# SwiGLU feed-forward on one core: chunks 1 to 3 computed together, each gate and up weight block loaded once for three matmuls, full array in place of column pairs

## The chip, the core and the metric

The kernel runs on one core of a Trainium2 chip. TensorE (PE) multiplies; a weight load (PEld) puts a stationary block into its array, a matmul streams up to 512 columns past it. ScalarE (ACT) computes the SiLU, VectorE (DVE) the products and most copies, SyncE (SP) issues nearly all transfers. The metric is the device time of one execution in microseconds; before the change it is 120.16 us (median of 3 runs, 119.78 to 120.52).

## What is computed

`out = (silu(x @ w_gate) * (x @ w_up)) @ w_down`, in bf16 with fp32 sums, for 2048 tokens, a model width D of 512 and an inner width F of 1376:

```python
B, S, D, F = 1, 2048, 512, 1376
g = _silu(x @ w_gate)      # (2048, 1376)
u = x @ w_up               # (2048, 1376)
return (g * u) @ w_down    # (2048, 512)
```

## The kernel before

**Tiles.** Tokens come in four chunks of 512, the inner width in ten blocks of 128 and a rest of 96. A *group* is one result of 128 inner columns by one chunk's 512 tokens, held in one of the 8 PSUM banks and summed over four matmuls (D is four blocks of 128, index `dk`). Kind G is a gate block, U an up block. X (one for each chunk) holds the last 96 gate columns and the last 32 up columns; Y (one for a pair of chunks) holds 64 more up columns of two chunks. That makes 20 G and U groups and one X for each chunk, then two Y: 86 groups. The down projection follows, with groups O, one for each 128 tokens.

**Banks.** Groups are numbered in order and group n uses bank n mod 8. Before TensorE starts a group it waits until every reader of group n - 8 is done (`free`).

**Column pairs.** `whole` issues one matmul of a group. At the start it uses the full array: one load of 128x128 and one matmul. From the fifth group on, `in_pairs` is true, and the work is issued as two halves side by side: two loads of 128x64 at column positions 0 and 64, two matmuls, each with half of the outputs and the same moving data. The Y groups use such halves too (L432), and the down projection (L470) uses four strips of 32 rows side by side. The rest of the last four token tiles (L506) is in the full array again: one load and one matmul of 128x128 for each inner block.

**Order on TensorE.** Warm-up matmuls, transposes of the first two token tiles, the first 8 groups (chunk 0, inner blocks 0 to 3) in slices of 128 and 256 tokens as x arrives, then the groups in number order: the rest of chunk 0, its X, chunk 1 (20 groups and X), chunk 2, chunk 3, both Y. Then the down projection starts. Its quads are four O groups each: a quad's step is four strip matmuls with different rows of the inner dimension. `strips(0, 0, ...)` runs ten such steps on the first four O groups, `strips(1, 0, ...)` the same on the next four. At its start a quad waits for the four banks to be free: those of the first quad were last used by groups 78 to 81 of 86, those of the second by 82 to 85.

**Readers.** For each pair (chunk, block), ACT writes silu(G) to `sg_sb` and DVE multiplies that by U into `hT_sb`. An X group has three readers: ACT writes 32 rows to `sgx_sb` and 64 rows to `sgy_sb`, and DVE makes `hx_sb` from `sgx_sb`. A Y group is read by one DVE product, which needs `sgy_sb` of both of its chunks. ACT and DVE each run their operations in the order in which they were planned.

**Transfers.** SP issues, in this order, a tile of x, the gate and up slabs with two transposing loads of x for the second half of chunk 0 among them, then one transposing load (`DMA_TRANSPOSE`, L95) for each of chunks 1, 2 and 3, then w_down. TensorE waits for chunk c's load before its first group of chunk c (`gu_needs`).

Of the kernel before, what the change touches and what calls it, by code (L numbers as in the profile page):

```python
# [14 lines left out]
def bass_standalone__swiglu_ffn__prompt_kernel(nc, x, w_gate, w_up, w_down, out):  # L15
    _, S, D = x.shape
    F = w_gate.shape[1]
    P = 128
    KD = D // P
    NFF = F // P  # L20
    NFT = NFF + 1
    F_LAST = F - NFF * P
    SC = 512
    NSC = S // SC
# [5 lines left out]
    HT = SC // 2  # L30
    NXN = HT // P
    NB = 8
    NSG = 4
    NOS = 8
    SR = 32
    PW = 64
# [2 lines left out]
    Y_ROWS = [0, 64, 0, 64]  # L39
    X_ROWS = [64, 0, 96, 32]  # L40
    ORDER = [1, 2, 3, 0]
    assert D == 512 and S % SC == 0 and KD == 4 and F_LAST == 96 and NSC % 2 == 0

    xf = x[0]
# [3 lines left out]
    UPH = F + 32  # L48
    WTOT = 2 * F
    XC0 = NFF * P  # L50
    YC0 = UPH + NFF * P

    with ExitStack() as es:
# [7 lines left out]
        hT_sb = sb("hT_sb", [P, NFF, S], BF16)  # L61
# [3 lines left out]
        adummy = sb("act_dummy", [P, 8], FP32)  # L65
        sg_sb = [sb(f"sg_sb{i}", [P, SC], FP32) for i in range(NSG)]
        sgx_sb = [sb(f"sgx_sb{c}", [P, SC], FP32) for c in range(NSC)]
# [10 lines left out]
        s_P = sem("s_P")  # L78
# [70 lines left out]
        groups = []  # L149
# [3 lines left out]
        def add_group(kind, **what):  # L153
            g = dict(kind=kind, at=len(groups), bank=banks[len(groups) % NB], readers=[], **what)
            groups.append(g)
            return g

        def add_op(eng, g, **what):
            n_read[eng] += 1
            op = dict(g=g, at=n_read[eng], **what)  # L160
            (act_ops if eng == "A" else dve_ops).append(op)
            g["readers"].append((eng, op["at"]))
            return op

        def tview(i, dk):
            return banks[KD * i + dk][:, 0:P // 2].bitcast(BF16)

        sg_reader = []
        n_sg = 0
        h_ready = {}  # L170

        def plan_pair(c, ft):
            nonlocal n_sg
            gg = add_group("G", c=c, ft=ft)
            gu = add_group("U", c=c, ft=ft)
            b = n_sg % NSG
            free = sg_reader[n_sg - NSG] if n_sg >= NSG else 0
            a = add_op("A", gg, kind="silu", out=sg_sb[b][:, :], src=gg["bank"][:, :], free=free)
            d = add_op(
                "D", gu, kind="mul", out=hT_sb[:, ft, c * SC:(c + 1) * SC], a=sg_sb[b][:, :],  # L180
                b=gu["bank"][:, :], after=a["at"],
            )
            sg_reader.append(d["at"])
            h_ready[c] = d["at"]
            n_sg += 1

        def yblk(c):
            return (0, 64) if c % 2 == 0 else (64, 128)
# [4 lines left out]
        def plan_x(c):  # L193
            g = add_group("X", c=c)
            y0, y1 = yblk(c)
            add_op("A", g, kind="silu", out=sgx_sb[c][96:128, :], src=g["bank"][64:96, :], free=0)
            a = add_op("A", g, kind="silu", out=sgy_sb[c // 2][y0:y1, :], src=g["bank"][0:64, :], free=0)
            d = add_op(
                "D", g, kind="mul", out=hx_sb[X_ROWS[c]:X_ROWS[c] + SR, c, :],
                a=sgx_sb[c][96:128, :], b=g["bank"][96:128, :], after=a["at"] - 1,  # L200
            )
            y_after[c // 2] = a["at"]
            t_ready[c] = d["at"]
# [10 lines left out]
        for i in range(NXN):  # L214
            for dk in range(KD):
# [3 lines left out]
                    out=xT_sb[:, dk, i * P:(i + 1) * P], src=tview(i, dk), stored=(None, 0),  # L219
                )  # L220
                xt_ready[i, dk] = (eng, op["at"])

        for c in range(NSC):
            for ft in range(NFF):
                plan_pair(c, ft)
            plan_x(c)
        for pi in range(NSC // 2):
            plan_y(pi)
# [3 lines left out]
        n_store = [0] * NOS  # L232
        tiles = [c * TPC + q for q in range(TPC) for c in ORDER]
        for at, t in enumerate(tiles):
            ob = at % NOS
            if at == 2 * TPC:
                parted = add_op(
                    "D", dict(readers=[]), kind="copy", ready=(s_T, N_TURNS), out=part_sb[:, :],
                    src=banks[(NO + NST - 1) % NB][:, LASTH:D], stored=(None, 0),
# [4 lines left out]
            for c0, c1 in parts:  # L244
                g = add_group("O", t=t, c0=c0, c1=c1)
# [66 lines left out]
        def on_tensor(pe):  # L312
            landed = set()

            def need(name, count=1):
                if name not in landed:
                    pe.wait_ge(loads[name], 16 * count)
                    landed.add(name)
# [3 lines left out]
            def after(eng, n):  # L322
                if n > read[eng]:
                    pe.wait_ge(s_A if eng == "A" else s_D, n)
                    read[eng] = n

            def free(g):
                if g["at"] >= NB:
                    for eng, n in groups[g["at"] - NB]["readers"]:
                        after(eng, n)  # L330

            in_pairs = False

            def whole(bank, dk, col, c, n0, n1):
                if not in_pairs:
                    return pe.matmul(  # L336
                        bank[:, n0:n1], lhsT=w_sb[:, dk, col:col + P],
                        rhs=xT_sb[:, dk, c * SC + n0:c * SC + n1], start=(dk == 0), stop=(dk == KD - 1),
                    )
                for y0 in (0, PW):  # L340
                    ins = pe.matmul(  # L341
                        bank[y0:y0 + PW, n0:n1], lhsT=w_sb[:, dk, col + y0:col + y0 + PW],
                        rhs=xT_sb[:, dk, c * SC + n0:c * SC + n1], start=(dk == 0), stop=(dk == KD - 1),
                        tile_position=(0, y0), skip_group_check=True,
                    )
                return ins

            def gu_needs(g, n0, n1):
                c, ft = g["c"], g["ft"]
                if c > 0:  # L350
                    need(f"x{c}")
                if c == 0 and n1 > HT:
                    need("x0b")
                if c == 0 and n1 > HT + P:
                    need("x0c")
                need(("wg" if g["kind"] == "G" else "wu") + str(slab_of[ft]))

            def gu_step(g, dk, n0, n1):
                c = g["c"]
                col = (0 if g["kind"] == "G" else UPH) + g["ft"] * P  # L360
                if c == 0:
                    for i in range(n0 // P, min(n1 // P, NXN)):
                        after(*xt_ready[i, dk])
                ins = whole(g["bank"], dk, col, c, n0, n1)
                if n1 == SC and dk == KD - 1:
                    ins.then_inc(s_P, 1)

            def gu_matmuls(g, n0, n1):
                if g["c"] == 0:
                    for i in range(n0 // P, min(n1 // P, NXN)):  # L370
                        after(*xt_ready[i, 0])
                gu_needs(g, n0, n1)
                for dk in range(KD):
                    gu_step(g, dk, n0, n1)
# [29 lines left out]
                for g in first[0:2]:  # L404
                    gu_step(g, dk, P, HT)
            for at in (2, 3, 4, 6, 5, 7):
                in_pairs = at >= 4
                gu_matmuls(first[at], 0, HT)
            for n0, n1 in ((HT, HT + P), (HT + P, SC)):
                for g in first[0:2]:  # L410
# [2 lines left out]
                gu_matmuls(g, HT, SC)  # L413

            for g in groups[NB:NO]:
                free(g)
                kind = g["kind"]
                if kind in "GU":
                    gu_matmuls(g, 0, SC)
                elif kind == "X":  # L420
                    c = g["c"]
                    need(f"wg{slab_of[NFF]}")
                    need("wut")
                    for dk in range(KD):
                        ins = whole(g["bank"], dk, XC0, c, 0, SC)
                    ins.then_inc(s_P, 1)
                elif kind == "Y":
                    need(f"wu{slab_of[NFF]}")
                    for dk in range(KD):
                        for c in (2 * g["pi"], 2 * g["pi"] + 1):  # L430
                            y0, y1 = yblk(c)
                            ins = pe.matmul(  # L432
                                g["bank"][y0:y1, :], lhsT=w_sb[:, dk, YC0:YC0 + 64],
                                rhs=xT_sb[:, dk, c * SC:(c + 1) * SC],
                                start=(dk == 0), stop=(dk == KD - 1),
                                tile_position=(0, y0), skip_group_check=True,
                            )
                    ins.then_inc(s_P, 1)
# [8 lines left out]
            def strips(q, k, fks, start, stop, turn=True):  # L447
# [7 lines left out]
                for fk in fks:  # L455
                    if fk == NFF:
                        need("wdt", 2 + TPC)
                    for c, g in zip(ORDER, quad):
                        t = g["t"]
# [38 lines left out]
            for g in groups[NO + TPC * (TPC - 1):]:  # L498
# [6 lines left out]
                for fk in full[1:]:  # L505
                    ins = pe.matmul(  # L506
                        g["bank"][:, 0:c1 - c0], lhsT=hT_sb[:, fk, t * P:(t + 1) * P],
                        rhs=wd_sb[:, fk, c0:c1], start=(rest and fk == 1), stop=(fk == NFF - 1),
                        skip_group_check=True,
                    )  # L510
# [3 lines left out]
        on_gpsimd(nc.gpsimd)  # L514
        on_scalar(nc.scalar)
        on_tensor(nc.tensor)
        on_vector(nc.vector)

# [27 lines left out]
```

## Time and profile before

| | |
|---|---|
| median of 3 runs | 120.16 us (119.78 to 120.52) |
| the profiled execution | 120.42 us, of which the span of instructions is 119.1 us |
| TensorE matmul busy | 116.2 us, 98% of the span |
| TensorE weight load busy | 63.5 us, 53% |
| VectorE, ScalarE busy | 38.8 us, 35.1 us |
| matmul records on the line of the pairs (L341) | 720, 71.1 us |

A record of a matmul lasts from its start to the modelled arrival of its last result, so consecutive matmuls overlap in the records: 0.379 us is the record of a 512-column matmul. How fast they follow each other is read from starts: the length of a merged row less one record, divided by the number of steps.

### The profile page before, as it was taken

The numbers are of one execution on the slowest core, as the hardware profiler recorded it, in microseconds if no ns is written. First come the engines' busy times: TensorE is split into PE (matmuls) and PEld (weight loads), VectorE is DVE, ScalarE is ACT, GpSimd is POOL, SyncE is SP. The second block draws the span as 40 slices with busy tenths as digits, with TensorE's granted clock in tenths as the row PEclk, the third lists the DMA queues.
The fourth block names the chain that finished last, engine by engine and source line by source line (L and its number), as shares of the span: only waits on it lengthen the run. The fifth ranks groups of instructions, "written<-read, shape, count | busy, mean of one in ns | idle before, by whom it ended". The sixth has DMA issues, their size and how long they took to land.

```text
span 119.1 us, 3076 instructions
## 1 busy us (share of the span) xinstructions
PE 116.2 (98%) x1385; PEld 63.5 (53%) x1386; DVE 38.8 (33%) x62; ACT 35.1 (29%) x62; POOL 0.5 (0%) x5
## 2 busy tenths in 40 slices
PE   7999999999999999999999999999999999999993
PEld 2999555555555555555555555544444444444463
DVE  0204634444334444344353344361000044004322
ACT  3406443262442363432454423430000033002121
POOL 1000000000000000000000000000000000000000
DMA  4999989995000000000000000000000015300522
GB/s 92 281 197 336 262 175 99 263 331 155 6 0 0 0 6 0 0 3 3 6 0 0 0 0 6 0 0 0 6 0 6 0 47 196 115 6 0 194 76 88
DMA packets 17533, 8.78 MB, mean 74 GB/s; under 512 B 10608, under 2 KB 17520, under 8 KB 17520
## 3 DMA queue, kind: packets, MB, share of 16 engines
q1 hardware_dynamic: 16704, 8.23, 28.9%
q10 hardware_dynamic: 816, 0.36, 1.1%
q8 instruction: 11, 0.18, 0.6%
q14 instruction: 2, 0.02, 0.0%
HBM read 4.65 MB, written 2.10 MB: 57 GB/s over the span
## 4 chain that ended last, share of the span: by engine, by line
PE 98%; issue 0%; DVE 0%
PE bank L341 60%; PE bank L470 25%; PE bank L506 7%; PE bank L378 2%; PE bank L336 2%; PE bank L432 1%; PE bank L388 1%; DVE o_sb L307 0%
## 5 line engine op out<-in xcount | busy, mean ns | idle before, releaser
L341 PE MATMUL bank<-xT_sb,w_sb 128*64 128x512 bf16 (+2 forms) x720 | 71.1, 360 | 0.0
L341 PEld LDWEIGHTS bank<-xT_sb,w_sb 128*64 128x64 bf16 x720 | 39.6, 110 | 31.2 <-issue 0.2
L302 DVE TENSOR_TENSOR hT_sb<-sg_sb,bank 128x512 bf16<-128x512 f32 x40 | 27.5, 688 | 40.6 <-PE bank L341 39.7
L294 ACT ACTIVATE sg_sb<-bank 128x512 f32<-128x512 f32 x40 | 23.8, 596 | 41.0 <-PE bank L341 40.9
L470 PE MATMUL bank<-wd_sb,hT_sb 32*128 32x512 bf16 x496 | 28.8, 374 | 0.0
L470 PEld LDWEIGHTS bank<-wd_sb,hT_sb 32*128 32x128 bf16 x496 | 12.7, 93 | 14.2 <-issue 0.4
L294 ACT ACTIVATE o_sb<-bank 128x512 bf16<-128x512 f32 (+1 forms) x8 | 4.2, 568 | 33.0 <-PE bank L470 27.8
L309 DVE CAST o_sb<-bank 128x512 bf16<-128x512 f32 x8 | 5.3, 688 | 21.2 <-PE bank L470 17.3
L506 PE MATMUL bank<-wd_sb,hT_sb 128*128 128x512 bf16 (+3 forms) x62 | 7.8, 286 | 0.2 <-issue 0.2
L506 PEld LDWEIGHTS bank<-wd_sb,hT_sb 128*128 128x128 bf16 x63 | 4.6, 98 | 3.7 <-issue 0.4
L470 PE MATMUL bank<-wd_sb,hy_sb 32*128 32x512 bf16 x32 | 4.6, 374 | 0.0
L378 PE MATMUL bank<-const-bfloat16-1.0 128*128 128x128 bf16 (+1 forms) x11 | 3.1, 455 | 0.8 <-PEq L531 0.8
L302 DVE TENSOR_TENSOR hx_sb<-sgx_sb,bank 32x512 bf16<-32x512 f32 x4 | 2.8, 692 | 3.5 <-ACT sgx_sb L294 3.5
L294 ACT ACTIVATE sgx_sb<-bank 32x512 f32<-32x512 f32 x4 | 2.4, 588 | 4.5 <-PE bank L341 4.5
L309 DVE COPY part_sb<-bank 128x256 f32<-128x256 f32 x1 | 0.4, 426 | 8.2 <-PE bank L470 8.2
L470 PE MATMUL bank<-wd_sb,hx_sb 32*128 32x512 bf16 x16 | 3.0, 374 | 0.0
L336 PE MATMUL bank<-xT_sb,w_sb 128*128 128x128 bf16 (+1 forms) x24 | 2.9, 294 | 0.0
L378 PEld LDWEIGHTS bank<-const-bfloat16-1.0 128*128 128x128 bf16 x11 | 1.4, 143 | 2.2 <-issue 2.2
L336 PEld LDWEIGHTS bank<-xT_sb,w_sb 128*128 128x128 bf16 x24 | 2.5, 130 | 0.1
L294 ACT ACTIVATE sgy_sb<-bank 64x512 f32<-64x512 f32 x4 | 2.4, 589 | 0.1
L309 DVE COPY xT_sb<-bank 128x128 bf16<-128x128 bf16 x4 | 0.9, 224 | 4.3 <-PE bank L388 4.3
L432 PE MATMUL bank<-xT_sb,w_sb 128*64 128x512 bf16 x16 | 1.9, 379 | 0.0
(15 smaller groups left out, 10.1 us busy)
## 6 DMA issues: line engine op xcount, KB each, us to landing
out_dram<-o_sb SPq DMA_DIRECT2D x15, 128.0 KB, 1.8
wd_sb<-in_w_down_dram SPq DMA_DIRECT2D x1, 1280.0 KB, 7.6
w_sb<-in_w_gate_dram SPq DMA_DIRECT2D x1, 480.0 KB, 5.5
w_sb<-in_w_up_dram SPq DMA_DIRECT2D x1, 448.0 KB, 7.5
w_sb<-in_w_gate_dram SPq DMA_DIRECT2D x1, 384.0 KB, 4.2
w_sb<-in_w_up_dram SPq DMA_DIRECT2D x1, 384.0 KB, 4.6
w_sb<-in_w_up_dram SPq DMA_DIRECT2D x2, 128.0 KB, 3.2
w_sb<-in_w_gate_dram SPq DMA_DIRECT2D x1, 256.0 KB, 3.7
```

The costliest lines, as they stand in the source:

```text
L294: act.activation(op["out"], op["src"], fn).then_inc(s_A, 1)
L302: ins = dve.tensor_tensor(op["out"], op["a"], op["b"], ALU.mult)
L309: ins = dve.tensor_copy(op["out"], op["src"])
L336: return pe.matmul(bank[:, n0:n1], lhsT=w_sb[:, dk, col:col + P], rhs=xT_sb[:, dk, c * SC + n0:c * SC + n1], start=(dk == 0), stop=(dk == ...
L341: ins = pe.matmul(bank[y0:y0 + PW, n0:n1], lhsT=w_sb[:, dk, col + y0:col + y0 + PW], rhs=xT_sb[:, dk, c * SC + n0:c * SC + n1], start=(dk ...
L378: pe.matmul(banks[NB - 1][:, 0:width], lhsT=ones_w, rhs=ones_m[:, 0:width], start=True, stop=True)
L388: ins = pe.matmul(tview(i, dk)[y0:y0 + width, :], lhsT=xn_sb[:, i, dk * P + y0:dk * P + y0 + width], rhs=ident[:, :], start=True, stop=Tru ...
L432: ins = pe.matmul(g["bank"][y0:y1, :], lhsT=w_sb[:, dk, YC0:YC0 + 64], rhs=xT_sb[:, dk, c * SC:(c + 1) * SC], start=(dk == 0), stop=(dk == ...
L470: ins = pe.matmul(g["bank"][:, :], lhsT=h, rhs=wd_sb[r0:r0 + SR, w, :], start=(start and fk == fks[0]), stop=(stop and fk == fks[-1]), til ...
L506: ins = pe.matmul(g["bank"][:, 0:c1 - c0], lhsT=hT_sb[:, fk, t * P:(t + 1) * P], rhs=wd_sb[:, fk, c0:c1], start=(rest and fk == 1), stop=( ...
```

## The change

1. G and U of chunks 1 to 3 are planned in sets: for each inner block, three G groups (chunks 1, 2, 3), then three U groups. Then come the three X groups one after the other, then both Y. Chunk 0 is as before.
2. TensorE runs a set with `dk` outside and the chunk inside: for each `dk`, the first matmul loads the weights, and the second and third are issued as an instruction without a weight load (`ldweights=False`) on the weights in the array. X is done likewise.
3. Before a set TensorE waits for the banks of all three groups, and for x of all three chunks.
4. `in_pairs` stays false: chunk 0 from its fifth group on, and chunks 1 to 3, use the full array. Y and the down projection are unchanged.
5. There are 6 buffers `sg_sb` for 4.

```diff
-    NSG = 4
+    NSG = 6
+    HELD = [1, 2, 3]
...
+        def plan_set(cs, ft):
+            ggs = [add_group("G", c=c, ft=ft) for c in cs]
+            gus = [add_group("U", c=c, ft=ft) for c in cs]
+            for c, gg, gu in zip(cs, ggs, gus):
...
-        for c in range(NSC):
-            for ft in range(NFF):
-                plan_pair(c, ft)
+        for ft in range(NFF):
+            plan_set([0], ft)
+        plan_x(0)
+        for ft in range(NFF):
+            plan_set(HELD, ft)
+        for c in HELD:
             plan_x(c)
...
+            def held_matmul(out, lhsT, rhs, start, stop, tile_position=(0, 0), skip_group_check=False):
+                ins = mybir.InstMatmult(
+                    name=nc.get_next_instruction_name(), engine=mybir.EngineType.PE, ldweights=False,
+                    start_tensor_calc=start, stop_tensor_calc=stop, ins=[pe.lower_ap(rhs), pe.lower_ap(lhsT)],
+                    outs=[pe.lower_ap(out)], tile_position=tile_position, tile_size=(P, lhsT.shape[1]),
+                )
+                return pe.add_instruction(ins)
...
             for at in (2, 3, 4, 6, 5, 7):
-                in_pairs = at >= 4
                 gu_matmuls(first[at], 0, HT)
...
             for g in groups[NB:NO]:
+                kind = g["kind"]
+                if g.get("c", 0) > 0:
+                    if g["c"] != HELD[0]:
+                        continue
+                    together = groups[g["at"]:g["at"] + len(HELD)]
+                    for h in together:
+                        free(h)
+                    if kind != "X":
+                        for h in together:
+                            gu_needs(h, 0, SC)
+                        col = (0 if kind == "G" else UPH) + g["ft"] * P
+                    else:
+                        col = XC0
+                    for dk in range(KD):
+                        for h in together:
+                            ins = whole(h["bank"], dk, col, h["c"], 0, SC, held=h is not g)
+                            if dk == KD - 1:
+                                ins.then_inc(s_P, 1)
+                    continue
                 free(g)
```

More of the change, by code (lines that the diff above doesn't have):

```diff
@@ L170, in bass_standalone__swiglu_ffn__prompt_kernel @@
         h_ready = {}
-        def plan_pair(c, ft):
+        def plan_set(cs, ft):
             nonlocal n_sg
[L174 to L185, printed above, removed]
+            ggs = [add_group("G", c=c, ft=ft) for c in cs]
+            gus = [add_group("U", c=c, ft=ft) for c in cs]
+            for c, gg, gu in zip(cs, ggs, gus):
+                b = n_sg % NSG
+                free = sg_reader[n_sg - NSG] if n_sg >= NSG else 0
+                a = add_op("A", gg, kind="silu", out=sg_sb[b][:, :], src=gg["bank"][:, :], free=free)
+                d = add_op(
+                    "D", gu, kind="mul", out=hT_sb[:, ft, c * SC:(c + 1) * SC], a=sg_sb[b][:, :],
+                    b=gu["bank"][:, :], after=a["at"],
+                )
+                sg_reader.append(d["at"])
+                h_ready[c] = d["at"]
+                n_sg += 1
         def yblk(c):
@@ L332, in on_tensor, with whole @@
             in_pairs = False
-            def whole(bank, dk, col, c, n0, n1):
+            def held_matmul(out, lhsT, rhs, start, stop, tile_position=(0, 0), skip_group_check=False):
[3 more added lines that the diff above has]
+                    outs=[pe.lower_ap(out)], tile_position=tile_position, tile_size=(P, lhsT.shape[1]),
+                )
+                return pe.add_instruction(ins)
+            def whole(bank, dk, col, c, n0, n1, held=False):
+                matmul = held_matmul if held else pe.matmul
                 if not in_pairs:
-                    return pe.matmul(
+                    return matmul(
                         bank[:, n0:n1], lhsT=w_sb[:, dk, col:col + P],
@@ L340, in whole @@
                 for y0 in (0, PW):
-                    ins = pe.matmul(
+                    ins = matmul(
                         bank[y0:y0 + PW, n0:n1], lhsT=w_sb[:, dk, col + y0:col + y0 + PW],
@@ L415, in on_tensor @@
             for g in groups[NB:NO]:
+                kind = g["kind"]
[17 more added lines that the diff above has]
+                    continue
                 free(g)
-                kind = g["kind"]
                 if kind in "GU":
```

## The prediction

> **What bounds the kernel now.** First the shares of the engines, then the chain that ended last (columns: start, length in us, what, number of instructions).
>
> ```profile
> PE 116.2 (98%) x1385; PEld 63.5 (53%) x1386; DVE 38.8 (33%) x62; ACT 35.1 (29%) x62; POOL 0.5 (0%) x5
> ```
>
> ```profile
> 7.12 70.99 PE bank L341 x720
> 78.11 1.73 PE bank L432 x16
> 79.84 29.46 PE bank L470 x544
> ...
> 109.46 7.80 PE bank L506 x62
> ```
>
> From 7.12 us on the chain never leaves TensorE. The 71 us on L341 are the gate and up work that the change rebuilds. A busy PE may still have holes between its matmuls, so the pace decides. It comes from rows of the order of time, each a stretch of equal matmuls (start, length, number), and from the durations of single records in the groups by shape.
>
> ```profile
> 29.81 4.48 PE L341 MATMUL bank<-xT_sb,w_sb 128*64 128x512 bf16 x40
> ```
>
> ```profile
> 109.46 5.78 PE L506 MATMUL bank<-wd_sb,hT_sb 128*128 128x512 bf16 x26 [0.16 <-issue]
> ```
>
> ```profile
> L341 PE MATMUL bank<-xT_sb,w_sb 128*64 128x512 bf16 x608 | 65.8, 379 | 0.0
> L341 PEld LDWEIGHTS bank<-xT_sb,w_sb 128*64 128x64 bf16 x720 | 39.6, 110 | 31.2 <-issue 0.2
> L506 PE MATMUL bank<-wd_sb,hT_sb 128*128 128x512 bf16 x26 | 5.8, 379 | 0.2 <-issue 0.2
> L341 PE MATMUL bank<-xT_sb,w_sb 128*64 128x256 bf16 x80 | 4.7, 273 | 0.0
> L506 PEld LDWEIGHTS bank<-wd_sb,hT_sb 128*128 128x128 bf16 x63 | 4.6, 98 | 3.7 <-issue 0.4
> ...
> L341 PE MATMUL bank<-xT_sb,w_sb 128*64 128x128 bf16 x32 | 1.1, 219 | 0.0
> ```
>
> Pairs: 40 records are 20 pairs, so (4.48 - 0.38)/19 = 0.2158 us for 512 columns. Full array, one load for each matmul: (5.78 - 0.38)/25 = 0.216 us. The two are equal, and in both the load (110 and 98 ns) lies beside the matmul before it: the slot has 216 ns. So the weight loads, 53% of the span in the first row, cost nothing here. There is nothing on the path for a saved load to give back, unless the slot itself shrinks.
>
> **The change part by part.**
>
> *Full array in place of pairs, chunk 0.* Chunk 0's short slices have to be checked too: pairs first, then full array, 256 and 128 columns.
>
> ```profile
> 9.71 2.68 PE L341 MATMUL bank<-xT_sb,w_sb 128*64 128x256 bf16 x46
> ...
> 8.93 0.95 PE L341 MATMUL bank<-xT_sb,w_sb 128*64 128x128 bf16 x28
> ```
>
> ```profile
> 6.63 0.49 PE L336 MATMUL bank<-xT_sb,w_sb 128*128 128x256 bf16 x3
> ...
> 116.11 0.61 PE L506 MATMUL bank<-wd_sb,hT_sb 128*128 128x128 bf16 x8
> ```
>
> By the groups above a record is 0.27 us for 256 columns and 0.22 us for 128. 256: pairs (2.68 - 0.27)/22 = 0.110, full (0.49 - 0.27)/2 = 0.110. 128: pairs (0.95 - 0.22)/13 = 0.056, full (0.61 - 0.22)/7 = 0.056. Cost: 0.
>
> *The change of shape moves.* Where pairs follow full-array work, and where strips follow halves, the trace has an extra step:
>
> ```profile
> 6.74 0.38 PE L336 MATMUL bank<-xT_sb,w_sb 128*128 128x256 bf16 x2
> 7.05 0.30 PE L341 MATMUL bank<-xT_sb,w_sb 128*64 128x256 bf16 x2
> ```
>
> ```profile
> 77.94 1.89 PE L432 MATMUL bank<-xT_sb,w_sb 128*64 128x512 bf16 x16
> 79.77 0.40 PE L470 MATMUL bank<-wd_sb,hT_sb 32*128 32x512 bf16 x4
> ```
>
> The last full-array matmul starts at 6.74 + 0.38 - 0.27 = 6.85, the pairs at 7.05: 0.20 where 0.11 is the pace, so 0.09 us for the switch. The change takes it away at 7 us and adds one of the same kind ahead of Y. Net 0, but chunk 0 ends 0.09 us earlier, which counts below. The Trainium skill, "TensorEngine Tiling (Array Packing)", section Key Properties, says that changing the tiling mode drains TensorE; the 0.09 us agrees, and by that rule the number of switches, hence the sum, is the same.
>
> *168 matmuls without a load* (20 sets x 4 x 2, and 4 x 2 for X). The trace has none, so bounds. Above: 0.2158 us as now. Below: 512 columns at the marginal pace. From 256 to 512 columns a slot grows by 0.2158 - 0.1095 = 0.1063 us, so 512 at that rate are 0.2126, and about 0.003 us of a slot doesn't scale. If that is the swap of weights, 168 x 0.003 = 0.5 us goes. I take 0: the strips show the same slot with four loads and four matmuls in it, so the fixed part doesn't follow the number of loads:
>
> ```profile
> 79.77 2.34 PE L470 MATMUL bank<-wd_sb,hT_sb 32*128 32x512 bf16 x40
> ```
>
> Ten quads, (2.34 - 0.38)/9 = 0.218 us with the switch's first step in it. The Trainium skill, "TensorE: Matmul & The Clock Gate", section "Wait — 56ns, not 53.3ns?", calls about 2.5 ns a fixed cost of every warm matmul; by that rule the 168 matmuls give 0, and were it the swap, 0.4 us. The traced slots agree with its size, but not one of them is without a load.
>
> *Sets need all three chunks of x at once.* Chunk 1 began alone; now chunk 3's load gates it too (start, length of issue; then the transfers issued in that stretch with the median time to landing, here of one).
>
> ```profile
> 23.34 0.60 PE L341 MATMUL bank<-xT_sb,w_sb 128*64 128x512 bf16 x4
> ```
>
> ```profile
> 18.08 3.52 SPq L95 DMA_TRANSPOSE xT_sb<-in_x_dram  x1
> ```
>
> ```profile
> xT_sb<-in_x_dram SPq DMA_TRANSPOSE x1, 6.0
> ```
>
> The first row is chunk 0's last pair at 23.34 and chunk 1's first at 23.55. With the switch gone TensorE is ready at 23.46. The third transpose on SP, chunk 3's, is issued at 18.08 and lands 6.0 later, at 24.08; the change leaves SP's list as it is. TensorE, with all later work behind it, waits 24.08 - 23.46 = **0.62 us**. Before, this load had until about 60 us. Bounds: 0 if it lands half a microsecond earlier, 0.9 if 0.3 later. w_down, issued behind it, isn't needed before 79 us.
>
> *Banks and readers within sets.* A set is 12 x 0.2158 = 2.59 us, G and U together 5.18 us. In that time ACT has three records of 0.60 us and DVE three of 0.69 us (2.1 us):
>
> ```profile
> L302 DVE TENSOR_TENSOR hT_sb<-sg_sb,bank 128x512 bf16<-128x512 f32 x40 | 27.5, 688 | 40.6 <-PE bank L341 39.7 <-ACT sg_sb L294 0.9
> L294 ACT ACTIVATE sg_sb<-bank 128x512 f32<-128x512 f32 x40 | 23.8, 596 | 41.0 <-PE bank L341 40.9
> ```
>
> A set waits for banks of groups 8 back: the latest is the first member of the set two before, which ended 2.59 us earlier and needs one operation (0.69). Covered with 1.8 us to spare. The 6 buffers `sg_sb` reach back two inner blocks: covered as well.
>
> *The end of the sets.* Now the readers of three X and two Y come in one burst, and the second quad of the down projection needs the banks of X2, X3, Y0 and Y1. What such readers take:
>
> ```profile
> 23.76 0.59 ACT L294 ACTIVATE sgx_sb<-bank 32x512 f32<-32x512 f32 x1 [1.13 <-PE bank L341]
> 24.38 0.59 ACT L294 ACTIVATE sgy_sb<-bank 64x512 f32<-64x512 f32 x1
> 24.87 0.58 ACT L294 ACTIVATE sg_sb<-bank 128x512 f32<-128x512 f32 x1
> ```
>
> ```profile
> 78.15 0.59 ACT L294 ACTIVATE sgx_sb<-bank 32x512 f32<-32x512 f32 x1 [1.13 <-PE bank L341]
> ...
> 78.84 0.69 DVE L302 TENSOR_TENSOR hx_sb<-sgx_sb,bank 32x512 bf16<-32x512 f32 x1 [0.86 <-ACT sgx_sb L294]
> 79.56 1.28 DVE L302 TENSOR_TENSOR hy_sb<-sgy_sb,bank 128x512 bf16<-128x512 f32 x2
> ```
>
> Let the X set start at 0. X1's last matmul is the tenth: it starts at 9 x 0.2158 = 1.94 and ends at 2.32, and ACT begins 0.04 later (23.34 + 0.38 to 23.76), at 2.36. From sgx to sgy it is 0.62 us, from sgy to the next 0.49. The fifth operation, X3's sgx, starts at 2.36 + 2 x (0.62 + 0.49) = 4.58 and ends at 5.17. The product hx follows 0.10 later (78.74 to 78.84), at 5.27, the first Y product 0.72 after that at 5.99, and both take 1.28: 7.27. Say 0.05 for the release: **7.32**. TensorE meanwhile: the X set 2.59, a switch 0.09, Y to the strips 79.77 - 77.94 = 1.83, ten quad steps 10 x 0.2158 = 2.16: ready for the second quad at **6.67**. It waits 0.65 us. If the step from sgy to the next sgx is 0.62 as the other way round, two steps add 0.26: 0.91. The rows have no sgx behind an sgy; sgy ahead of sg is the nearest (0.49), but sgx writes other partitions than it reads, as sgy of chunk 1 does, and it is behind such an operation that I see 0.62. I take the middle, **0.78 us**. Before, only one X had to be read: the Y products ended at 80.84 and the second quad came at 81.93, with 1.1 us to spare. The first quad waits for the three U products and X1's hx, done at 3.7; it starts at 4.51. Covered.
>
> **Sum:** 0 + 0 + 0 + 0.62 + 0.78 = +1.40 us. Nothing behind takes it back: the down projection runs at its pace on TensorE to the end. Against the profiled execution, 120.42 us (span 119.1, 1.3 around it), this is 121.8, with a span of 120.5; against the median of 120.16, which is 0.26 lower, **121.5 us**.
>
> **The rivals.**
>
> *The slot shrinks.* Matmuls without a load run at 0.213: 0.5 us back, 121.0. For it, nothing in this trace has such a matmul; against it, the strips.
>
> *x is there in time.* Not slower by what can be told: if chunk 3's load lands by 23.46, the first wait is gone, at its place at the start of the first set, and 121.5 - 0.62 = 120.9 is left, within 1%. It decides at 0.6 us, a tenth of the load's own 6.0 us, and the five transposing loads differ by more than that (of all five, from issue to landing):
>
> ```profile
> DMA to landing us min/median/max: 3.1/6.0/8.3
> ```
>
> With the shrunk slot too it is 120.4.
>
> *The load of the next set comes into view.* With three matmuls to one load, the load might not slip beside the last matmul that still uses the old weights. 84 loads (80 for G and U, 4 for X) of 98 ns are 8.2 us: 129.7. Against it: the rows of L506, where each load lies beside a matmul in the same full array. The Trainium skill, "TensorE: Matmul & The Clock Gate", section "The mechanism", says that a load overlaps running matmuls only in other row groups; the 0.216 us of L506 contradicts that.
>
> *The matmuls get their loads all the same.* The records would show 360 loads for 192; time as in the sum.
>
> *A gain beyond 1%*, the other side outright, would need 1.2 us more than nothing, and the rows leave 0.5.
>
> **How the numbers follow.** 1% (1.2 us) is about what a measurement of this kernel tells from no change. Forecast as summed, 121.0 to 122.2: 0.62. Slot shrinks: 0.12. x in time: 0.14. Loads in view: 0.06. Unforeseen, half of it a gain: 0.06. The range runs from 120.4 (both mild rivals) to 122.3 (waits of 0.9 each less rounding, and the 0.36 us by which single runs differ from the median). It leaves out the loads in view, the unforeseen and some edges. The line at 1% is 121.36, just below the forecast: slower takes 0.40 of the forecast's 0.62, 0.03 of the shrunk slot, 0.01 of x in time, the 0.06 and half of the unforeseen: 0.52. Faster 0.04, within 1% the rest, 0.44.
>
> **What would show it.** The loads on the gate and up lines fall from 720 to 192, with no other pace: 0.216 us in chunk 0 and in the sets (0.213 for the rival, over 0.24 for loads in view). TensorE idles about 0.6 us near 23.5 us, ended by a transfer, and about 0.8 us some 6.7 us after the X set begins, ended by DVE's product of Y. Both Y products follow a row of six ACT operations without a gap. I am wrong if TensorE has no hole at one of the two places, or if a hole is followed by a slower pace.

## The result and the profile after

| | before | after |
|---|---|---|
| median | 120.31 us (6 runs, 119.78 to 120.52) | 121.3 us (6 runs, 121.01 to 121.44) |
| ratio | | 1.0085, 95% interval 1.0061 to 1.0108 |
| the profiled execution | 120.42 us, span 119.1 | 121.40 us, span 120.1 |
| loads on the gate and up lines | 744 (720 of them halves) | 216 |

The kernel is slower by 1.0 us, 0.85%. The forecast was 121.5 us in a range of 120.4 to 122.3. The shares of the engines, on the page of the kernel after:

```profile
PE 116.2 (97%) x1018; PEld 44.0 (37%) x858; DVE 37.0 (31%) x62; ACT 33.1 (28%) x62; POOL 0.5 (0%) x5
```

TensorE's matmuls take the 116.2 us that they took before; the busy time of the weight loads fell from 63.5 to 44.0 us, and the kernel did not get faster by it. The groups by shape, of the kernel after: L345 is the matmul without a load, L350 the one with it.

```profile
L345 PE MATMUL bank<-xT_sb,w_sb 128*128 128x512 bf16 x165 | 49.3, 379 | 0.2
...
L350 PEld LDWEIGHTS bank<-xT_sb,w_sb 128*128 128x128 bf16 x216 | 20.7, 102 | 52.2 <-issue 45.6
```

(165 of the 168 have a record.) The 216 loads are the 192 of the forecast and the 24 of the first slices. The order of time on TensorE at the start of the sets, in the kernel after:

```profile
22.88 1.03 PE L350 MATMUL bank<-xT_sb,w_sb 128*128 128x512 bf16 x3
23.75 0.59 PE L345 MATMUL bank<-xT_sb,w_sb 128*128 128x512 bf16 x2
24.18 0.38 PE L350 MATMUL bank<-xT_sb,w_sb 128*128 128x512 bf16 x1
24.39 0.59 PE L345 MATMUL bank<-xT_sb,w_sb 128*128 128x512 bf16 x2
24.82 0.38 PE L350 MATMUL bank<-xT_sb,w_sb 128*128 128x512 bf16 x1
```

Two things are to be read here. The starts 24.18, 24.39 and, 0.59 - 0.38 later, 24.60, then 24.82 are 0.21 to 0.22 us apart. Rounding leaves open whether that is 0.216 or the rival's 0.213, so a long stretch has to decide. The sets and X use 84 weight blocks, each with one load and three matmuls; the first block starts at 23.53 (below), the last one, X's fourth, in this row:

```profile
77.27 0.38 PE L350 MATMUL bank<-xT_sb,w_sb 128*128 128x512 bf16 x1
```

(77.27 - 23.53)/(83 x 3) = 0.2158 us: a matmul without a load takes the slot of one with it. And there is no hole at the start of the sets: the first set starts at 22.88 + 1.03 - 0.38 = 23.53, right behind chunk 0, so the wait for chunk 3's x is missing. That load came sooner than in the profile before (issue, then issue to landing):

```profile
17.81 2.09 SPq L96 DMA_TRANSPOSE xT_sb<-in_x_dram  x1
```

```profile
xT_sb<-in_x_dram SPq DMA_TRANSPOSE x1, 4.4
```

It landed at 22.2 us, against 24.0 before. The other wait did come. The rows of TensorE at the second quad of the kernel after, then the chain that ended last through it (from the chain's pieces in order of time), then DVE's last X product from the order of time:

```profile
79.86 2.34 PE L501 MATMUL bank<-wd_sb,hT_sb 32*128 32x512 bf16 x40
82.98 0.40 PE L501 MATMUL bank<-wd_sb,hT_sb 32*128 32x512 bf16 x4 [0.78 <-DVE hy_sb L307]
```

```profile
77.69 0.59 ACT sgx_sb L299
78.30 0.59 ACT sgy_sb L299
78.91 0.59 ACT sgx_sb L299
79.52 0.59 ACT sgy_sb L299
80.14 0.59 ACT sgx_sb L299
80.75 0.60 ACT sgy_sb L299
81.55 1.30 DVE hy_sb L307 x2
82.98 27.38 PE bank L501 x504
110.52 7.80 PE bank L537 x62
```

```profile
80.83 0.69 DVE L307 TENSOR_TENSOR hx_sb<-sgx_sb,bank 32x512 bf16<-32x512 f32 x1 [0.53 <-ACT sgx_sb L299]
```

Ten quad steps from 79.86 end at 82.03; the second quad starts at 82.98, **0.95 us** late. (The 0.78 in brackets counts from the end of the last record, which lies 0.17 behind that step.) In the profile before, the chain never left TensorE from 7.12 us on; here it leaves it once, for six ACT operations with 0.02 us from one to the next and the two Y products of DVE, and comes back. What the Y products waited for last is DVE's own X product: it ended at 81.52, 0.03 before they started, and the last ACT operation had ended at 81.35. Everything behind the hole is shifted: the last stage starts at 110.52 where it started at 109.46, 1.06 later. Of that 0.95 is the hole; the strips had already started 0.09 later (79.86 for 79.77). The rows are rounded, which leaves 0.01 to 0.02 us on each of these differences.

### The profile page after: what moved, and what is told of

Its sections match the earlier page's. It is cut to its first block, busy times and chain, and to the rows that moved or that the text cites. A ratio compares the mean times of both kernels' runs of the same rounds, so it can differ in the third digit from the quotient of the medians.

```text
span 120.1 us, 2200 instructions
## 1 busy us (share of the span) xinstructions
PE 116.2 (97%) x1018; PEld 44.0 (37%) x858; DVE 37.0 (31%) x62; ACT 33.1 (28%) x62; POOL 0.5 (0%) x5
## 4 chain that ended last, share of the span: by engine, by line
PE 93%; ACT 3%; DVE 1%; issue 1%; DVEq 0%
PE bank L350 31%; PE bank L345 30%; PE bank L501 23%; PE bank L537 6%; PE bank L392 2%; ACT sgy_sb L299 1%; ACT sgx_sb L299 1%; DVE hy_sb L307 1%; PE bank L402 1%; DVE o_sb L312 0%; DVEq L306 0%
## 5 line engine op out<-in xcount | busy, mean ns | idle before, releaser
L350 PE MATMUL bank<-xT_sb,w_sb 128*128 128x512 bf16 (+2 forms) x212 | 50.3, 338 | 0.2
L345 PE MATMUL bank<-xT_sb,w_sb 128*128 128x512 bf16 x165 | 49.3, 379 | 0.2
L350 PEld LDWEIGHTS bank<-xT_sb,w_sb 128*128 128x128 bf16 x216 | 20.7, 102 | 52.2 <-issue 45.6
L307 DVE TENSOR_TENSOR hT_sb<-sg_sb,bank 128x512 bf16<-128x512 f32 x40 | 25.7, 684 | 44.6 <-PE bank L350 44.2
L299 ACT ACTIVATE sg_sb<-bank 128x512 f32<-128x512 f32 x40 | 21.7, 598 | 44.7 <-PE bank L350 44.6
L501 PEld LDWEIGHTS bank<-wd_sb,hT_sb 32*128 32x128 bf16 x496 | 14.4, 93 | 13.4 <-issue 1.7
```

The lines of the kernel that those rows point to most:

```text
L299: act.activation(op["out"], op["src"], fn).then_inc(s_A, 1)
L307: ins = dve.tensor_tensor(op["out"], op["a"], op["b"], ALU.mult)
L345: return pe.add_instruction(ins)
L350: return matmul(bank[:, n0:n1], lhsT=w_sb[:, dk, col:col + P], rhs=xT_sb[:, dk, c * SC + n0:c * SC + n1], start=(dk == 0), stop=(dk == KD ...
L501: ins = pe.matmul(g["bank"][:, :], lhsT=h, rhs=wd_sb[r0:r0 + SR, w, :], start=(start and fk == fks[0]), stop=(stop and fk == fks[-1]), til ...
```

## The experiments

Theory A: the order of the sets is the whole loss, through TensorE's waits that it brings, and neither the full array nor the matmuls without a load change the time. Theory B: one of these two has a price or a gain of its own.

### The X groups ahead of the last set

```diff
-        for ft in range(NFF):
+        for ft in range(NFF - 1):
             plan_set(HELD, ft)
         for c in HELD:
             plan_x(c)
+        plan_set(HELD, NFF - 1)
```

> The changed kernel with one thing moved: the three X groups are planned and run ahead of the last gate and up set (inner block 9) and not behind it. The same work, the same loads, the same matmuls without a load. Theory A (the whole loss is the 0.95 us that TensorE waits at the second quad of the down projection, for the readers of three X and two Y in a burst): that hole is gone, and the time is 121.3 - 0.95 = 120.35 us, level with the kernel before (120.3). Theory B (full array or the matmuls without a load cost something by themselves): the hole goes, but the time stays 0.4 us or more above the kernel before. If the set ahead of it now waits for ACT, a new hole shows at the U set of block 9 or at the first quad (the U products of block 9 end only about 0.1 us before the strips ask for them).

Measured: 120.58 us, ratio to before 1.002 (0.9999 to 1.0041). The burst of readers is the same, but now ACT works through it beside a set, from 72.65 to 76.3 us. The second quad follows the first without a hole: the row of strips below has 56 records, that is 14 quad steps at one pace, from the first strip on (this kernel's order of time).

```profile
79.25 0.81 PE L464 MATMUL bank<-xT_sb,w_sb 128*64 128x512 bf16 x6
80.02 3.20 PE L502 MATMUL bank<-wd_sb,hT_sb 32*128 32x512 bf16 x56
```

The hole was most of the loss: of 0.99 us above the kernel before, 0.36 us are left in the medians. The ratio doesn't tell them from nothing, but its interval reaches 0.5 us, and 0.36 lies between theory A's nothing and theory B's 0.4 us or more. This run alone does not decide between the two theories; the next two do, by taking B's candidates one at a time. Part of the 0.36 can be the start: in the profiled execution the slow pace at the very start lasted to 6.3 us, and chunk 0 ended at 23.67 us, for 5.8 and 23.43 in the profile of the full array alone below. But that is one execution, and over all ten profiles chunk 0's end lies anywhere from 23.0 to 24.0. The U products of block 9, the thinnest margin here, delayed the first strips by some 0.02 us.

### Every matmul of a set loads its weights

```diff
-                            ins = whole(h["bank"], dk, col, h["c"], 0, SC, held=h is not g)
+                            ins = whole(h["bank"], dk, col, h["c"], 0, SC, held=False)
```

> The changed kernel in its own order, but every matmul of a set loads its weights (360 loads for 192 on the gate and up lines). Theory A: a slot stays at 0.216 us with or without a load, so 121.3 us, within 0.1 us of the changed kernel, with the same hole of 0.95 us at the second quad. Rival (the 168 matmuls without a load save their fixed part): 0.4 to 0.5 us more than the changed kernel, 121.7 to 121.8.

Measured: 121.27 us, ratio to before 1.0096 (1.0072 to 1.012), where the changed kernel has 1.0085. Groups, then order of time, of this kernel:

```profile
L350 PEld LDWEIGHTS bank<-xT_sb,w_sb 128*128 128x128 bf16 x384 | 36.3, 98 | 36.9 <-DMA w_sb<-in_w_gate_dram 0.5
```

```profile
29.78 4.48 PE L350 MATMUL bank<-xT_sb,w_sb 128*128 128x512 bf16 x20
...
82.77 0.40 PE L501 MATMUL bank<-wd_sb,hT_sb 32*128 32x512 bf16 x4 [0.79 <-DVE hy_sb L307]
```

20 matmuls with 20 loads: (4.48 - 0.38)/19 = 0.2158 us. The slot is the same with a load for each matmul and with one for three, and the hole is the same, so the rival of the shrunk slot is gone. The times agree, 121.27 and 121.3, but the two intervals together would still let 0.4 us through; it is the slot that decides.

### The full array alone

```diff
             for at in (2, 3, 4, 6, 5, 7):
-                in_pairs = at >= 4
                 gu_matmuls(first[at], 0, HT)
```

> The kernel before with one line of the change: full array in place of column pairs in all four chunks, each matmul with its load; the order of chunks, X and Y as before. Theory A: the slot is 0.216 us either way and the 0.09 us of the change of shape only moves, so 120.3 us, no difference from before (within 0.15 us). Theory B (the full array costs): 120.7 us or more.

Measured: 120.2 us, ratio 1.0004 (0.9986 to 1.0022). Pairs and full array cost the same, within 0.3 us either way by the interval; the switch that goes at 7 us comes back ahead of Y. The second quad again follows without a hole (order of time of this kernel):

```profile
79.76 2.77 PE L469 MATMUL bank<-wd_sb,hT_sb 32*128 32x512 bf16 x48
```

### The order of the sets alone, with column pairs

The changed kernel with all loads (as above) and with `in_pairs = at >= 4` put back.

> The changed kernel's order (sets of three chunks, three X, then Y) with the column pairs of the kernel before and a load for each half. Theory A (order alone is the loss): 121.3 us, with the hole of 0.9 to 1.0 us at the second quad and none elsewhere. Theory B (order costs nothing, full array or missing loads do): 120.3 us.

Measured: 121.8 us, ratio 1.0144 (1.0114 to 1.0174). The order alone makes the loss, as theory A has it, but more of it than the 121.3 expected, and not only at the place named. TensorE at the start of the sets and at the second quad:

```profile
22.38 0.81 PE L355 MATMUL bank<-xT_sb,w_sb 128*64 128x512 bf16 x6
23.78 0.62 PE L355 MATMUL bank<-xT_sb,w_sb 128*64 128x512 bf16 x4 [0.59 <-DMA xT_sb<-in_x_dram]
```

```profile
83.27 0.40 PE L502 MATMUL bank<-wd_sb,hT_sb 32*128 32x512 bf16 x4 [0.91 <-DVE hy_sb L307]
```

Here is the first wait of the prediction: chunk 0 was through at 23.03, x of chunk 3 landed at 23.65, and the set started at 23.78, 0.75 us late. And the second hole is longer, 0.91 for 0.78 in the same count. With pairs there is no switch ahead of Y, so TensorE is at the second quad 0.09 us sooner, while the readers are not: that makes 0.09 of the 0.13, and in the changed kernel that switch is hidden in the hole behind it. By the count from the step's end, as in the changed kernel, this hole is 1.07 us; 0.75 and 1.07 make 1.8, for 1.6 us (1.4 to 2.1 by the interval) measured.

### Chunk 3's x behind w_down

The changed kernel; SP issues w_down's big load ahead of chunk 3's transposing load.

```diff
-            for c in range(1, NSC):
+            for c in range(1, NSC - 1):
                 load_x(sp, f"x{c}", c * SC, (c + 1) * SC)
             sp.dma_start(
                 wd_sb[:, 0:NFF, :], w_down[0:NFF * P, :].rearrange("(k p) d -> p k d", p=P)
             ).then_inc(load_sem("wd"), 16)
+            load_x(sp, f"x{NSC - 1}", (NSC - 1) * SC, S)
```

> The changed kernel with chunk 3's transposing load of x issued behind w_down's big load instead of ahead of it. It tests the first wait of the prediction, which did not come in the changed kernel's profile (x of chunk 3 landed at 22.2 us, the first set was due at 23.5). If the set really waits for the latest of the three loads, TensorE stands from about 23.5 us until that load lands, at the earliest 4 us later than before (w_down landed at 27.8), so 4 to 6 us, and the time is 125 to 127.5 us; the wait of 0.95 us at the second quad is unchanged. If something else gates the first set, the hole is under 1 us and the time stays at 121.3 to 121.7.

Measured: four executions of 125.9 to 128.1 us, median 127.6; the two shorter ones give a ratio of 1.0501 (1.0414 to 1.0587). The mean granted clock was 0.986 in the two shorter ones and 0.973 in the two longer, and the profile is of one of the longer (128.09 us). TensorE in it, then stretches of it, the second of them inside the first (length, TensorE busy with the number of its records, granted clock, transfers):

```profile
22.62 0.81 PE L351 MATMUL bank<-xT_sb,w_sb 128*128 128x512 bf16 x3
27.63 0.58 PE L351 MATMUL bank<-xT_sb,w_sb 128*128 128x512 bf16 x1 [4.20 <-DMA xT_sb<-in_x_dram]
```

```profile
23.00:27.60 4.60, 0.43 (x2) 0.84 1.07 211
26.00:26.50 0.50, 0.00 (x0) 0.59 1.27 290
27.60:32.70 5.10, 5.07 (x12) 0.50 0.15 41
32.70:60.00 27.30, 27.30 (x127) 1.00 0.00 1
```

The first set does wait for the latest of the three loads: due at 23.27, started at 27.63, 4.4 us. And in this execution the price of the wait is more than its length: behind it the granted clock is 0.50 for 5 us, in which 12 matmuls run in place of 24, some 2.6 us more. In the two shorter executions the loss of mean clock is half as large (0.014 for 0.027), so this price is not fixed. Behind the hole of 0.95 us in the changed kernel there is no such thing: its granted clock is 1.00 throughout. The Trainium skill, "TensorE: Matmul & The Clock Gate", section "Part 1: The HAM clock gate", puts the border at an idle window of about 3.4 us and has the clock fall to a half. The half agrees with the 0.50. The length does not: the clock was 1.00 up to 26.0 us and 0.59 on average in the half microsecond after it, so it fell at about 26.1, 2.7 us after the end of the last matmul's record (23.43), and this measurement decides. No run here has a wait between these lengths.

### Pairs in sets, X groups ahead of the last set

The order of sets alone with column pairs, and the move of X of the first experiment: of the two waits only the first can be left.

> The sets in the new order with column pairs and all loads, and with the X groups ahead of the last set, so that only the first wait (for x of chunk 3) can be left. Theory A2 (with the sets' order there are two waits, the burst of readers and, in the kernels with pairs, chunk 3's x, which landed at 23.65 and 24.04 us in the two profiles with pairs and at 22.2 to 23.5 in those without): 121.8 - 1.07 = 120.7 us, and the profile shows a hole of 0.3 to 0.8 us at 23 us and none at the second quad. Rival (the kernel with pairs in sets loses 0.5 us elsewhere): no hole at 23 us and still 120.7.

Measured: 120.53 us, ratio 1.0017 (0.9982 to 1.0051), 0.2 us under the number expected, and not told apart from before. The profile has the wait at 23 us, which decides against the rival, and it is shorter than in the kernel with pairs and X last (order of time of this kernel); the second quad has none.

```profile
22.57 0.81 PE L356 MATMUL bank<-xT_sb,w_sb 128*64 128x512 bf16 x6
23.60 0.62 PE L356 MATMUL bank<-xT_sb,w_sb 128*64 128x512 bf16 x4 [0.22 <-DMA xT_sb<-in_x_dram]
```

So the first wait is real, but its length goes with the landing in the profile at hand: 0.75 us there, 0.39 here, none in the changed kernel. It was not quite the only one left: the first strips, at 79.99, come some 0.15 us later behind Y than in the changed kernel. They need the last U product of block 9, the third of the DVE row below, which ends 0.32 us before them (0.31 in the first experiment).

```profile
79.99 3.20 PE L503 MATMUL bank<-wd_sb,hT_sb 32*128 32x512 bf16 x56
```

```profile
77.79 1.88 DVE L308 TENSOR_TENSOR hT_sb<-sg_sb,bank 128x512 bf16<-128x512 f32 x3 [1.35 <-PE bank L356]
```

### Both kernels once more

> The kernel before once more, for one number: when chunk 3's x lands. If the pairs with their 720 loads (more instructions to fetch) delay it: 23.5 us or later. If the landing only scatters from run to run: anywhere from 22.2 to 24.1.

> The changed kernel once more, for the same number and for the waits: chunk 3's x at 22.2 to 23.1 us if the landing goes with the kernel, anywhere from 22.2 to 24.1 if it scatters; a hole at the first set only where it lands after about 23.4. The hole at the second quad 0.95 us again, since its length is that of a chain of eight operations and not of a transfer.

One execution each: 120.76 and 121.38 us. In the kernel before, chunk 3's x landed at 24.85, as expected if pairs delay it (23.5 or later) and outside the 22.2 to 24.1 of mere scatter. In the changed one it landed at 23.29, later than the 22.2 to 23.1 that was expected if the landing goes with the kernel, and still about 0.1 us ahead of the moment at which it would have held up the first set. The second quad's hole was 0.95 us again:

```profile
82.97 0.40 PE L501 MATMUL bank<-wd_sb,hT_sb 32*128 32x512 bf16 x4 [0.78 <-DVE hy_sb L307]
```

The landing in the second execution of the kernel before, from the issue of chunk 3's load (order of time, then issue to landing):

```profile
20.15 2.59 SPq L95 DMA_TRANSPOSE xT_sb<-in_x_dram  x1
```

```profile
xT_sb<-in_x_dram SPq DMA_TRANSPOSE x1, 4.7
```

So it was late here because it was issued late, at 20.15 for 18.08, and not because it took longer. Over the profiles with the load in its place, issue to landing is 6.0, 4.7, 4.6 and 5.2 us with pairs (the kernel before twice, sets with pairs, the same with X early), and 4.4, 4.7, 4.8, 4.6 and 4.5 in the full array: no clear difference. The landings are 23.5 to 24.9 with pairs and 22.2 to 23.5 without: the two ranges touch. In both kernels that were profiled twice the landing moved by 0.8 to 1.1 us from one execution to the next. So the landing scatters by more than the margin of the first wait, and whether the kernel shifts it as well is open.

## Why the prediction was right, and where its steps were not

- *Full array in place of pairs: 0.* Right: 1.0004 by itself.
- *The switch moves: 0.* Right in the sum. In the changed kernel the new one lies ahead of the hole and is hidden by it; what should have shown as 0.09 us gained in chunk 0 was only 0.02 in the profile (23.53 for 23.55), since the slow pace at the very start ended later in that execution, at 6.1 us for 5.8.
- *Matmuls without a load: 0 taken, 0.5 as the lower bound.* Right: 0.2158 us a slot with and without a load, and putting 168 loads back changed nothing that can be told. Its argument, that the fixed part of a slot doesn't follow the number of loads, holds. The fixed 2.5 ns of every warm matmul, in the section "Wait — 56ns, not 53.3ns?" of the Trainium skill's "TensorE: Matmul & The Clock Gate" cited there, stands for matmuls without a load too.
- *Wait for chunk 3's x: 0.62 us.* This is the step that failed: in the changed kernel the wait was 0 in both profiles. The prediction names a missing hole at one of its two places as a sign of being wrong, and this is that sign. The mechanism behind it holds, since the wait is there as soon as the load is late (0.75, 0.39 and 4.4 us in three other kernels); what failed is the input. The landing at 24.08 was taken over from one profile of the kernel before as if it belonged to the load; in the changed kernel it was 22.2 and 23.3, ahead of the 23.5 at which it is needed. The rival "x is there in time" is what came true; it had 0.14 and should have had more.
- *Wait at the second quad: 0.78 us, bounds 0.65 and 0.91.* Right place, right chain, right releaser; measured 0.95, just over the bound. The step from sgy to the next sgx was the long one each time (78.30 to 78.91: 0.61). The profile before had a row that says so, and the prediction overlooked it: sgy of chunk 1, which writes other partitions than it reads, and the next sg are 0.61 us apart there (rows in the last section). With it the sum takes 0.91 and not the middle. With the X set's start at 75.33 the Y products ended at 7.51, which is the upper bound's 7.53. The release was 82.98 - 82.84 = 0.14 us where I had said 0.05.
- *The sum: +1.40.* Measured +1.0 (0.73 to 1.30 by the interval). One wait of two came, at 0.95. The sum is too large, by one term's 0.62 less the other's 0.17. That 121.5 lies only 0.2 from 121.3 is luck in part: these two errors offset a little, and the base of 120.16, from three runs, became 120.31 with three more. The rival that came true, at 120.9, lies further off, because it has the same short second wait on the same base. The X groups moved ahead of the last set show where the loss is: without the second wait there is none that the measurement tells.
- *The chances.* The parts named for "slower" add up to 0.53, not 0.52.

No version beat the kernel before: with both waits out of the way the order of the sets is not told apart from it, since every slot was already full.

## What to carry to other kernels

Read the pace from the starts of matmuls before saving weight loads: where a load lies beside a 0.216 us slot, as here, taking it away gives nothing, though the loads were busy for 53% of the span. Batching groups that share weights also batches their readers and their inputs: count the burst at the end of the batch against the moment at which the next stage wants the same banks, and put the groups with the most readers ahead of the last batch. A transfer's landing time from one profile is not a constant: here it moved by 0.8 to 1.1 us between two executions of the same kernel, so a wait of half a microsecond that rests on it is a chance and not a term.

## What was not expected of the hardware

- Two ACT operations in a row follow each other in 0.49 us where both write the partitions that they read (the `sgy` and `sg` rows of chunk 0 quoted in the prediction), and in 0.61 us where one of them writes others: all five steps in the rows of ACT above. The nearest thing to a test is in the kernel before, where the same two shapes follow each other in both ways. `sgy` of chunk 1 writes rows 64 to 127 of its tile from rows 0 to 63 of the bank; `sgy` of chunk 2 writes the rows that it reads (order of time of that kernel, chunk 1 and then chunk 2):

```profile
42.50 0.59 ACT L294 ACTIVATE sgy_sb<-bank 64x512 f32<-64x512 f32 x1
43.12 0.60 ACT L294 ACTIVATE sg_sb<-bank 128x512 f32<-128x512 f32 x1
```

```profile
60.63 0.59 ACT L294 ACTIVATE sgy_sb<-bank 64x512 f32<-64x512 f32 x1
61.13 0.58 ACT L294 ACTIVATE sg_sb<-bank 128x512 f32<-128x512 f32 x1
```

  0.62 and 0.50 us by these rounded starts. In the first experiment `sgy` of chunk 3, which also writes other rows, is followed by `sg` in 0.61 us:

```profile
75.72 0.59 ACT L300 ACTIVATE sgy_sb<-bank 64x512 f32<-64x512 f32 x1
76.33 0.60 ACT L300 ACTIVATE sg_sb<-bank 128x512 f32<-128x512 f32 x1
```

  No experiment changed the partitions alone; these pairs differ in the chunk as well.
- The transposing load of chunk 2, ahead of chunk 3's on the same queue, takes 5.7 to 6.2 us in the four profiles with column pairs and 4.3 to 5.0 in the six with the full array; chunk 3's does not tell the kernels apart. Why was not tried: the kernels with pairs also have more instructions (3076 in the kernel before, 2200 after) and fetch more of them, 0.18 MB for 0.11 to 0.13, so the half-array work and the fetching are not told apart.
- TensorE went on 0.13 us after chunk 3's load had landed (23.65 to 23.78, 27.50 to 27.63) and 0.14 us after DVE's product had ended.
